# Retention's loads and steps put in another order, output zeros written later, token lists built in steps

## The chip, the core and the metric

One core of a Trainium2 chip runs the whole program. The metric is the device time of one execution in microseconds (us); of the kernel before three timed runs are at hand, and one profiled execution. The core has five engines that each take their instructions in order: TensorE (PE, with its weight loads PEld), VectorE (DVE), ScalarE (ACT), GpSimd (POOL) and SyncE (SP), which here only issues DMAs. Sixteen DMA engines move data.

## What is computed

Retention over 4 batches, 8 heads, 768 steps of 64 dimensions; its output, as 3072 rows of 512, goes through a soft mixture of 8 experts with 4 slots each, and then through a top-2 mixture of 8 experts. All is float32.

```python
for t in range(S):                                   # retention
    state = gamma * state + einsum('bhd,bhe->bhde', k[:, :, t], v[:, :, t])
    y[:, :, t] = scale * einsum('bhd,bhde->bhe', q[:, :, t], state)
x = y.transpose(0, 2, 1, 3).reshape(3072, 512)
# soft layer: logits x @ phi, softmax over tokens into slots, w1/relu/w2 per expert, softmax over slots back
# top-2 layer: noisy logits, the two largest per token, their softmax
for e in range(E):
    for k in range(2):
        mask = top2[:, k] == e
        out[mask] += top2_w[mask, k, None] * (relu(x[mask] @ w1[e]) @ w2[e])
```

## The kernel before

Retention works on 24 chunks of 128 steps, six for each batch. Loads go by pairs of chunks: `load_q` (L218) and `load_kv` (L232) move 512 KB each of q, k and v for chunk pair u; q goes into two of the four parts of `comp`, k and v into the four parts of `raws`. A load of k and v fills 128 partitions; its first 64 belong to the first chunk of the pair. `spread` (L241) copies k (ACT, two instructions of 64 partitions) and scales v (POOL, two) for one chunk. `k_t` transposes k on PE and ACT copies it to `kT`; `q_t` transposes half of a pair's q and DVE multiplies it with decay factors (two instructions); `qk` makes the scores (PE) and DVE masks them (`am`); `inter` is the product of q with the state `sbd`; `kv` updates the state (PE, then ACT copies it to `sbd`); `y_out` (the last product, L320) ends a chunk and DVE writes `XT`; `x_n` transposes it. `group0` to `group2` make the logits and slot sums for four chunks. `put` ties each step behind the one before it on PE, so the order in which the code calls the steps is the order on PE. On the other engines a list scheduler chooses the order when the kernel is built: each instruction has the priority of its place in the code and is placed when its operands and its slot are free by the scheduler's own reckoning; after that the order is fixed. `after(...)` ties instructions behind a given one on the same engine. A tile in a pool has a number of buffers (`bufs`); the next user of a buffer waits for the last accessor of the one before.

The loop over j (L438) takes chunk j, but k_t for chunk j + 2, spread for j + 3. In each step from j = 1 to 19 one or two quarters (512 KB) of the soft layer's W1 are requested on SP, each behind a one-element DVE copy from `XT[j - 1]` that paces it (L478); 28 quarters are the experts 0 to 6. In steps 11 to 16 a write of 1 MB of zeros each, from a zero tile `zt` in the buffer of W1's expert 6, clears `out` (L483). Ahead of the loop stand the loads in the order q(0), cta (356 KB of constants), kv(0), q(1), kv(1), q(2), kv(2), all on SP, with phi on ACT; `fill` issues PE products that nobody reads, 10 of them first and 2 + 2 around the first k_t.

After the loop W1 goes through PE (L536), W2's eight loads of 2 MB wait on SP for the buffers that this frees, and the products with W2 (L600) end the soft layer. Then the router makes the two choices per token (`sels`), their ranks `rr` and blocks `blk`. V1 and V2 are the weights of the top-2 layer (2 MB for each expert); three quarters of V1[2] are requested on ACT's queue behind the write of the router's weights (L695), the last quarter on SP behind a POOL copy (L979, L980).

The top-2 layer takes for each expert up to 6 full blocks of 128 tokens and one of 64, in three groups. `lists` (L747) makes the token list of one expert: comparisons on DVE, two products on POOL, 24 small matmuls (L762). `lists_all` makes the lists of experts 1 to 7 together in two passes i = 0, 1, each with a comparison table `oh` (three DVE instructions), a product `bta` on DVE and one on POOL, and 24 matmuls (L798). `fetch` gathers the tokens' rows (POOL, indirect DMA), `turn` transposes them, `hidden` makes the hidden values (PE L891, ACT relu L894, DVE rest L896 into `hhl`), `main` the output blocks of 24 matmuls (L924 to L926), evacuated by ACT into `yo` (three buffers, L933), and `add_rows` adds them to the rows of `out` with an indirect DMA on POOL (L905). Each add waits for the one before it, and the first for the zeros. `split_hi` and `split_lo` divide V2 into two parts (`wh` on ACT, `wl` on DVE). `HOOK` runs a function ahead of one matmul of one block: g_rest, the products with the last quarter of V1[2], at block 0 of expert 0, seventh step; the joint lists' two passes at blocks 1 and 2 of expert 0, where the gathers of expert 1 follow. V2[1] comes in quarters on SP, one after each of the first blocks (L944).

## Time and profile before

| | us |
|---|---|
| timed runs | 593.89, 594.40, 596.17 |
| median of the three | 594.40 |
| profiled execution | 598.08 |
| its span, first to last instruction | 596.2 |

| stage | from to, us |
|---|---|
| retention | 0 to 161 |
| soft layer's products | 161 to 204 |
| router, first list and gathers | 204 to 228.5 |
| expert 0 | 228.5 to 285.5 |
| experts 1 to 7 | 285.5 to 581 |
| last adds and end | 581 to 596 |

The page gives an engine's busy time over the whole span; the stages have different limits, so the table by stretches and the waits are read next. PE's clock has two levels here, 1.2 and 2.4 GHz; the profile gives it as a share of the higher, so 0.50 is the lower and a mean between the two says how long each was granted. An entry in square brackets behind an instruction says how long its engine stood idle before it and what ended that.

### The profile page before, as it was taken

What the parts mean: (1) busy time and instruction counts of PE and PEld (TensorE: products, weight loads), DVE (VectorE), ACT (ScalarE), POOL (GpSimd) and SP (SyncE); (2) the same over time, 40 slices, a digit from 0 to 9 for tenths busy, and PEclk for the clock granted to TensorE, in tenths of its full rate; (3) what the DMA queues carried; (4) which work ended last, traced back from release to release, by engine and by line L of the source; (5) the groups of instructions that cost most, each with busy time, mean ns of one, the idle gap of its engine ahead of it and who ended that gap; (6) DMA issues with size and microseconds to landing.
All of it is one profiled execution on the core that took longest, in us unless ns stands there. A gap on an engine that the chain in (4) does not pass through costs nothing. (4 is left out here: it accounts for less than half of the span.)

```text
span 596.2 us, 10652 instructions
## 1 busy us (share of the span) xinstructions
PE 551.9 (93%) x4176; PEld 418.9 (70%) x4176; DVE 254.6 (43%) x521; ACT 242.4 (41%) x529; POOL 224.0 (38%) x214
## 2 busy tenths in 40 slices
PE   6899999699899888799999999999999999999990
PEld 3787878578553345677787787787787787787870
DVE  3467777375303177834425225235235234324200
ACT  3565746344202235325426246256345345334200
POOL 3434634141103055445344434435344345432331
PEclk9799999799899898989999999999999999999996
DMA  9999999996699962446567566566656653644232
GB/s 251 246 273 308 236 323 379 349 349 236 257 384 410 379 211 68 96 96 167 131 138 186 109 146 181 109 149 181 128 141 174 133 122 55 138 101 51 38 40 33
DMA packets 79453, 111.76 MB, mean 187 GB/s; under 512 B 10034, under 2 KB 51570, under 8 KB 78498
## 3 DMA queue, kind: packets, MB, share of 16 engines
q1 hardware_dynamic: 65488, 94.75, 49.3%
q0 software_dynamic: 9696, 14.37, 17.4%
q10 hardware_dynamic: 4210, 1.87, 1.1%
q8 instruction: 35, 0.57, 0.4%
q14 instruction: 24, 0.20, 0.1%
HBM read 87.92 MB, written 20.41 MB: 182 GB/s over the span
## 5 line engine op out<-in xcount | busy, mean ns | idle before, releaser
L924 PE MATMUL pyc<-wh,hhl 128*128 128x512 f32 x384 | 154.1, 401 | 0.2 <-issue 0.2
L926 PE MATMUL pyc<-wh,hhl 128*128 128x512 f32 x384 | 152.4, 397 | 0.0
L925 PE MATMUL pyc<-wl,hhl 128*128 128x512 f32 x384 | 150.8, 393 | 0.0
L905 POOL DMA_INDIRECT out_dram<-yo,lsa x49 | 77.2, 1576 | 159.7 <-DMA out_dram<-yo,lsa 35.9
L896 DVE SCALAR_TENSOR_TENSOR hhl<-phc,hhl 128x512 fp32r<-128x512 f32 (+1 forms) x128 | 66.8, 551 | 73.9 <-ACT hhl L894 68.6
L926 PEld LDWEIGHTS pyc<-wh,hhl 128*128 128x128 f32 x384 | 72.4, 189 | 16.9
L925 PEld LDWEIGHTS pyc<-wl,hhl 128*128 128x128 f32 x384 | 72.6, 189 | 15.3
L924 PEld LDWEIGHTS pyc<-wh,hhl 128*128 128x128 f32 x384 | 72.3, 188 | 15.2 <-issue 0.8
L933 ACT ACTIVATE yo<-pyc,cg 128x512 f32<-128x512 f32 x48 | 33.0, 688 | 117.5 <-PE pyc L926 108.7
L872 DVE TENSOR_TENSOR wl<-w,wh 128x1024 fp32r<-128x1024 f32 x32 | 39.1, 1225 | 56.3 <-ACT wh L866 56.3
L894 ACT ACTIVATE hhl<-phc 128x512 fp32r<-128x512 f32 (+1 forms) x128 | 58.9, 515 | 10.2 <-PE phc L891 9.0
L838 POOL DMA_INDIRECT cg<-ctab,lsa x49 | 51.9, 1059 | 19.7 <-issue 13.5
L866 ACT CAST wh<-w 128x1024 fp32r<-128x1024 f32 x32 | 33.5, 1049 | 35.6 <-DMA w<-in_moe_w_dram 27.7
L296 DVE TENSOR_TENSOR am<-pa,cta 128x512 f32<-128x512 f32 x48 | 33.1, 692 | 31.3 <-PE py L320 15.9
L254 POOL TENSOR_TENSOR comp<-raws,cta 64x512 f32<-64x512 f32 x24 | 24.9, 1038 | 46.9 <-PE py L320 29.0
L274 DVE TENSOR_TENSOR qT<-pt,cta 64x512 f32<-64x512 f32 x48 | 33.0, 688 | 21.4 <-PE pt L269 21.0
L891 PE MATMUL phc<-cts,gs 128*128 128x256 f32 (+1 forms) x192 | 36.6, 300 | 3.0 <-DVE hhl L896 1.8
L254 POOL TENSOR_TENSOR vl<-raws,cta 64x512 f32<-64x512 f32 x24 | 24.9, 1038 | 34.7 <-PE py L320 22.4
L891 PEld LDWEIGHTS phc<-cts,gs 128*128 128x128 f32 x192 | 29.4, 191 | 10.3 <-issue 3.4
L292 PE MATMUL pa<-qT,kT 64*128 64x128 f32 x384 | 29.0, 292 | 1.2 <-ACT kT L283 1.2
L292 PEld LDWEIGHTS pa<-qT,kT 64*128 64x128 f32 x384 | 24.3, 194 | 5.6 <-issue 4.0
L310 PE MATMUL py<-qT,sbd 128*128 128x128 f32 x160 | 22.5, 285 | 4.9 <-ACT sbd L337 4.9
(191 smaller groups left out, 684.1 us busy)
## 6 DMA issues: line engine op xcount, KB each, us to landing
w<-in_moe_w_dram SPq DMA_DIRECT2D x77, 512.0 KB
w<-in_moe_w_dram SPq DMA_DIRECT2D x11, 2048.0 KB
comp<-in_q_dram SPq DMA_DIRECT2D x12, 512.0 KB
raws<-in_k_dram SPq DMA_DIRECT2D x12, 512.0 KB
raws<-in_v_dram SPq DMA_DIRECT2D x12, 512.0 KB
out_dram<-w SPq DMA_DIRECT2D x6, 1024.0 KB
gs<-gr SPq DMA_DIRECT2D x112, 32.0 KB
w<-in_moe_w_dram SPq DMA_DIRECT2D x2, 1024.0 KB
```

The source lines that it names most:

```text
L254: pool_ins[0] = nc.gpsimd.tensor_tensor(VL[j][rs], RAW[u][1][gs, :, r, :], gv[gs, r, t, :, None].to_broadcast([64, H, D]), op=OP.mult)
L292: mm = nc.tensor.matmul(pa[s][:, hp, :], KT[j][r, hp, :], QT[t][r, hp, g, :], start=True, stop=True)
L838: nc.gpsimd.indirect_dma_start(out=cg[:rows(b), i, :], out_offset=None, in_=ctab, in_offset=index(e, b, rows(b)))
L866: ins = nc.scalar.copy(wh, V2[e][:, 1024 * i:1024 * i + 1024])
L872: nc.vector.tensor_tensor(wl, V2[e][:, 1024 * i:1024 * i + 1024], WH[e][i], op=OP.subtract)
L891: nc.tensor.matmul(ph[:, w * i:w * i + w], GS[e][:, kf + i], CT[e, g][:, :w], start=True, stop=True)
L894: relu.append(nc.scalar.activation(h[:, :, :w], pv, AF.Relu))
L896: last = nc.vector.scalar_tensor_tensor(h[:, :, w + t0:w + t0 + 2 * P], pv[:, :, :2 * P], 0.0, h[:, :, :2 * P], op0=OP.max, op1=OP.subtract)
L905: nc.gpsimd.indirect_dma_start(out=out, out_offset=index(e, b, n), in_=y, in_offset=None, bounds_check=N - 1, oob_is_err=False, compute_op ...
L924: nc.tensor.matmul(py, hhl[:, kf, ts], wh, start=(kf == 0), stop=False)
L925: nc.tensor.matmul(py, hhl[:, kf, ts], wl, start=False, stop=False)
L926: nc.tensor.matmul(py, hhl[:, kf, tl], wh, start=False, stop=(kf == KF - 1))
```

## The change

Retention: the loads start with k, v of pair 0 in two halves of 64 partitions each (q(0) is issued between the first halves of k and v), then pair 1, then q(1); cta goes to ACT's queue, phi later. The four fills around the first k_t are dropped. Chunk 0 is run ahead of the loop through y_out, with qk(1) behind it; the loop begins at j = 1, takes k_t for chunk j + 1, spread for j + 2 and the k and v loads in the same place early in the step; steps 1 and 2 take both halves of a q pair. W1's quarters go over steps 3 to 20.

Zeros: the six writes leave the loop. `zt` is now a tile of 4 KB per partition, written by POOL; a one-element DVE operation on it reads the last gathered rows of expert 0; behind it one DMA on SP writes all of `out`.

V1[2]: its three quarters go to SP, behind an ACT copy that reads `wsl`.

Lists: expert 1 gets a list of its own by `lists`, behind the first hidden products, so its gathers no longer wait for the joint lists, which now serve experts 2 to 7. `lists_all` is cut into steps, one after each of the blocks 1 to 5 of expert 0 and 0 of expert 1; a one-element ACT copy from that block's `yo` into each tile (`mark`) holds the step's DVE instructions until then. Both `bta` products are on DVE. The two passes of matmuls go to block 4 of expert 0 and block 1 of expert 1, and the gathers of expert 2 follow the second.

```diff
-WP = 19
-Z0, ZN = 11, 6
+WP = 21
+W0, ZW = 3, 2 * DM
...
-        def load_kv(u):
+        def load_kv(u, part=None):
...
+            ps = slice(0, P) if part is None else slice(64 * part, 64 * part + 64)
...
+                nc.sync.dma_start(x[ps].rearrange("p h r d -> p h (r d)"),
+                                  src[b, :, 256 * t:256 * t + 256, :].rearrange("h (p r) d -> p h (r d)", r=2)[ps])
+                if u == 0 and part == 0 and src is k:
+                    load_q(0)
...
-        load_q(0)
-        nc.sync.dma_start(cta, csta)
-        load_kv(0)
-        nc.scalar.dma_start(phis, phi.rearrange("(k p) s -> p k s", p=P))
+        nc.scalar.dma_start(cta, csta)
+        load_kv(0, 0)
+        load_kv(0, 1)
+        load_kv(1)
         load_q(1)
-        load_kv(1)
         spread(0)
+        put(k_t, 0)
         for s in range(2):
             put(q_t, 0, s)
-        fill(psA, "py", FU)
-        put(k_t, 0)
-        fill(psA, "py", FV)
         load_q(2)
         spread(1)
         load_kv(2)
+        nc.scalar.dma_start(phis, phi.rearrange("(k p) s -> p k s", p=P))
         put(qk, 0)
         put(k_t, 1)
+        put(inter, 0)
+        put(kv, 0)
+        put(y_out, 0)
         spread(2)
-        put(q_t, 1, 0)
-        for j in range(NCH + 1):
+        put(qk, 1)
+        for j in range(1, NCH + 1):
             t, g = divmod(j, 2)
             if j < NCH:
 
+                if j + 1 < NCH:
+                    put(k_t, j + 1)
                 if j + 2 < NCH:
-                    put(k_t, j + 2)
+                    spread(j + 2)
+                if g and t + 3 < NT:
+                    load_kv(t + 3)
                 put(inter, j)
-                tn, s = (t + 1, 1) if g == 0 else (t + 2, 0)
-                if tn < NT:
-                    put(q_t, tn, s)
+                qs = [(1, 0), (1, 1)] if j == 1 else [(2, 0), (2, 1)] if j == 2 else [(t + 2, 0) if g else (t + 1, 1)]
+                for tn, s in qs:
+                    if tn < NT:
+                        put(q_t, tn, s)
...
-                if Z0 <= j < Z0 + ZN:
-                    with after(w_dma):
-                        a = NCH // ZN * (j - Z0)
-                        nc.sync.dma_start(ov[:, a:a + NCH // ZN, :],
-                                          zt[:, None, :].to_broadcast([P, NCH // ZN, DM]))
...
+            for i in range(28 * (j - W0) // (WP - W0), 28 * (j + 1 - W0) // (WP - W0)) if W0 <= j < WP else ():
+                s, dst, src = load_w1(i)
+                nc.vector.tensor_copy(dst[0:1, 0:1], XT[j - 1][0:1, 0, 0:1])
+                nc.sync.dma_start(dst, src)
...
         with after(put):
-            for i in range(KD - 1):
-                nc.scalar.dma_start(V1[2][:, 1024 * i:1024 * i + 1024], v1p[:, i])
+            nc.scalar.copy(V1[2].rearrange("p (k n) -> p k n", k=KD)[0:1, :KD - 1, 0:1], wsl[0:1, :KD - 1, 0:1])
+        for i in range(KD - 1):
+            nc.sync.dma_start(V1[2][:, 1024 * i:1024 * i + 1024], v1p[:, i])
...
     def lists_all():
+
+        def mark(ap, y):
+            nc.scalar.copy(ap, y[0:1, 0:1])
...
+        y = yield
         bm = cc.tile([P, NCH, E, LB], F16, name="bma", bufs=1)
+        mark(bm[0:1, 0, 0, 0:1], y)
...
-                eng = nc.gpsimd if a else nc.vector
-                eng.tensor_tensor(bt[:, :, a], bm, sb[:, a, :, :, None].to_broadcast([P, NCH, E, LB]), op=OP.mult)
+                mark(bt[0:1, 0, a, 0, 0:1], y)
+                nc.vector.tensor_tensor(bt[:, :, a], bm, sb[:, a, :, :, None].to_broadcast([P, NCH, E, LB]), op=OP.mult)
...
-        for e in range(1, E):
+        for e in range(2, E):
             LS[e] = ls[:, e]
+        for g in range(G):
+            fetch(2, g)
...
+            PACE.pop((e, b), tuple)(*[yo][:(e, b) in PACED])
...
+    PACED = (0, 1), (0, 2), (0, 3), (0, 4), (0, 5), (1, 0)
...
+            zt = cc.tile([P, ZW], I32, name="zt", bufs=1)
+            nc.gpsimd.memset(zt, 0)
+            nc.vector.tensor_single_scalar(zt[0:1, 0:1], CG[0, G - 1][0:1, 0, 0:1].bitcast(I32), 0, op=OP.bitwise_and)
+            nc.sync.dma_start(out.rearrange("(p a) d -> p (a d)", p=P).rearrange("p (a d) -> p a d", d=ZW),
+                              zt.bitcast(F32)[:, None, :].to_broadcast([P, N * DM // (P * ZW), ZW]))
...
+            lists(1, cc, psC, LB)
             gen = lists_all()
             next(gen)
-            HOOK[0, 1, 4] = next, gen
-            HOOK[0, 2, 2] = listed, gen
+            for b in PACED:
+                PACE[b] = gen.send
+            HOOK[0, 4, 4] = HOOK[1, 1, 2] = next, gen
...
-            pre[0] += [(fetch, e + 1, g) for g in range(G)] if e else []
+            pre[0] += [(fetch, e + 1, g) for g in range(G)] if e != 1 else []
```

## Rows read from the trace of the kernel before

**Rows 1.** Page, parts 1 and 2: engine totals; busy tenths in 40 slices
```profile
PE 551.9 (93%) x4176; PEld 418.9 (70%) x4176; DVE 254.6 (43%) x521; ACT 242.4 (41%) x529; POOL 224.0 (38%) x214
...
DMA  9999999996699962446567566566656653644232
```

**Rows 2.** Stretches: length; PE, PEld, DVE, ACT, POOL busy; clock, DMA share, GB/s
```profile
18.00:20.00 2.00, 2.00 (x14) 1.67 (x14) 0.74 (x2) 0.58 (x1) 1.87 (x3) 0.50 1.20 290
...
24.00:84.00 60.00, 58.83 (x793) 49.46 (x792) 42.19 (x81) 35.23 (x72) 27.14 (x28) 1.00 0.95 272
...
200.00:210.00 10.00, 8.79 (x72) 5.05 (x73) 3.78 (x12) 3.67 (x5) 0.09 (x1) 0.83 1.04 397
...
250.00:260.00 10.00, 7.89 (x40) 6.61 (x41) 7.02 (x21) 4.74 (x11) 1.87 (x2) 0.66 0.40 92
...
290.00:340.00 50.00, 50.00 (x254) 39.30 (x253) 16.56 (x35) 20.88 (x48) 22.39 (x18) 1.00 0.62 138
```

**Rows 3.** Who PE waited for: total us, times, longest (104:116, then 229.6:285.4)
```profile
PE py L310 <- ACT sbd L337: 4.9, 1, 4.9
...
PE pli L798 <- DVE bta L795: 2.1, 1, 2.1
...
PE phc L891 <- DVE hhl L896: 1.8, 1, 1.8
...
PE ptc L857 <- ACT cts L850: 1.4, 1, 1.4
```

**Rows 4.** Instructions in order of time: start, length; the start
```profile
6.53 2.81 DVE L274 TENSOR_TENSOR qT<-pt,cta 64x512 f32<-64x512 f32 x4 [4.41 <-PE pt L269]
...
8.68 2.51 ACT L253 COPY comp<-raws 64x512 f32<-64x512 f32 x4 [5.01 <-DMA raws<-in_k_dram]
...
22.05 1.65 PE L320 MATMUL py<-am,comp 128*64 128x128 f32 x16
...
32.69 1.05 PE L320 MATMUL py<-am,vl 128*64 128x128 f32 x16
```

**Rows 5.** Instructions in order of time; output products 7, 8, 15, 16
```profile
60.08 1.04 PE L320 MATMUL py<-am,vl 128*64 128x128 f32 x16
...
66.17 1.05 PE L320 MATMUL py<-am,comp 128*64 128x128 f32 x16
...
104.84 1.05 PE L320 MATMUL py<-am,vl 128*64 128x128 f32 x16
...
109.32 1.24 ACT L253 COPY comp<-raws 64x512 f32<-64x512 f32 x2 [5.39 <-DMA raws<-in_k_dram]
...
117.86 1.05 PE L320 MATMUL py<-am,comp 128*64 128x128 f32 x16
```

**Rows 6.** Instructions in order of time; end of the W2 products
```profile
198.70 1.06 PE L600 MATMUL po<-w,ht 128*32 128x512 f32 x8 [0.29 <-DMA w<-in_moe_w_dram]
```

**Rows 7.** Instructions in order of time; first list to the end of expert 1
```profile
218.58 1.58 PE L762 MATMUL pli<-bt,oh 128*128 128x14 f16 x24 [2.08 <-POOL bt L755]
...
228.50 0.97 PE L891 MATMUL phc<-cts,gs 128*128 128x256 f32 x6 [0.75 <-issue]
...
229.79 0.92 POOL L838 DMA_INDIRECT cg<-ctab,ls  x1 [0.30 <-issue]
...
235.72 0.64 PE L184 MATMUL pg<-w,sotT 128*32 128x256 f32 x8
...
241.26 1.94 POOL L905 DMA_INDIRECT out_dram<-yo,ls  x1 [4.34 <-ACT w L943]
...
250.33 1.04 ACT L866 CAST wh<-w 128x1024 fp32r<-128x1024 f32 x1 [5.62 <-DMA w<-in_moe_w_dram]
...
285.51 0.69 ACT L933 ACTIVATE yo<-pyc,cg 128x512 f32<-128x512 f32 x1 [0.34 <-PE pyc L926]
...
326.60 0.69 ACT L933 ACTIVATE yo<-pyc,cg 128x512 f32<-128x512 f32 x1 [0.35 <-PE pyc L926]
```

**Rows 8.** The chain that ended last: start, length, what
```profile
561.62 4.88 DMA out_dram<-yo,lsa
```

More of the change, by code (lines that the diff above doesn't have):

```diff
@@ L408, in load_w1 @@
         def load_w1(i):
-            if i % 4 == 0 and i // 4 not in W1:
+            if i % 4 == 0:
                 W1[i // 4] = (ringp if i < 8 else ringa).tile([P, 4096], F32, name="w", tag="w")
@@ L459 @@
                     put(qk, j + 1)
-                if j % 4 == 0 and j:
+                if j % 4 == 0:
                     put(group0, j // 4 - 1)
@@ L466 @@
                 put(y_out, j)
-                if j + 3 < NCH:
-                    spread(j + 3)
-                if g == 0 and t + 3 < NT:
-                    load_kv(t + 3)
-            if j:
-                if j == NCH - 3:
-                    load_w(W1, w1, E - 1, nc.sync, ringr)
-                if j == NCH - 2:
-                    load_w(W2, w2, 0, nc.sync, ringb)
-                for i in range(28 * (j - 1) // WP, 28 * j // WP if j <= WP else 0):
-                    s, dst, src = load_w1(i)
-                    nc.vector.tensor_copy(dst[0:1, 0:1], XT[j - 1][0:1, 0, 0:1])
-                    w_dma = nc.sync.dma_start(dst, src)
-                if Z0 <= j < Z0 + ZN:
-                    with after(w_dma):
-                        a = NCH // ZN * (j - Z0)
-                        nc.sync.dma_start(ov[:, a:a + NCH // ZN, :],
-                                          zt[:, None, :].to_broadcast([P, NCH // ZN, DM]))
-                if j == 8:
-                    with after(pool_ins[0]):
-                        load_small()
+            if j == NCH - 3:
+                load_w(W1, w1, E - 1, nc.sync, ringr)
+            if j == NCH - 2:
+                load_w(W2, w2, 0, nc.sync, ringb)
+            for i in range(28 * (j - W0) // (WP - W0), 28 * (j + 1 - W0) // (WP - W0)) if W0 <= j < WP else ():
+                s, dst, src = load_w1(i)
+                nc.vector.tensor_copy(dst[0:1, 0:1], XT[j - 1][0:1, 0, 0:1])
+                nc.sync.dma_start(dst, src)
+            if j == 8:
+                with after(pool_ins[0]):
+                    load_small()
         ictx.close()
@@ L800, in lists_all @@
                                  start=(i == 0 and c == 0), stop=(i == 1 and c == NCH - 1))
+            if i == 0:
+                y = yield
         lt = cc.tile([P, E, LB], F32, name="lta", bufs=1)
@@ L825 @@
     CG, HOOK = {}, {}
-    def listed(gen):
-        next(gen)
-        for g in range(G):
-            fetch(1, g)
     def fetch(e, g):
@@ L944, in main @@
                 nc.sync.dma_start(t[:, s], src[:, s])
-    feed = {}
+    feed, PACE = {}, {}
+    PACED = (0, 1), (0, 2), (0, 3), (0, 4), (0, 5), (1, 0)
     LAST = []
```

38 lines of the change are left out of this document (18 added, 20 removed).

## The prediction

> **What bounds the kernel now.** I read the page's engine totals first: TensorE (PE) is busy for 93% of the span and the 16 DMA engines are near full only in the first third [rows 1]. A change that takes no PE work away can therefore win only where PE stands still or runs at its lower clock, so I went on to the table by stretches [rows 2] and to the list of what PE waited for [rows 3]. From 24 to 84 us PE is busy 58.83 of 60 us at full clock: the retention loop is bound by PE, and ordering its steps anew is worth nothing there. The same holds from 290 us on, where 50 of 50 us are busy. Three places are left.
>
> The first is the start: chunk 0's output product begins only at 22.05 us [rows 4], and PE works at the lower level, 1.2 GHz, around 18 to 20 us [rows 2]. The second is one gap in chunk 16. ScalarE (ACT) sat 5.39 us for k's load, and since ACT takes its instructions in order, the copy into sbd stood behind it and PE waited 4.9 us for that [rows 3, 5]. Output products 15 and 16 are 13.02 us apart where 7 and 8, the same place in a group of four, are 6.09 apart: 6.9 us are lost. The third is expert 0 of the second layer: its last full block is evacuated at 285.51 and expert 1's at 326.60, a pace of 41.1 us [rows 7], while expert 0's first hidden product starts at 228.50, 57 us for the same blocks.
>
> The total is made against the profiled execution, 598.08 us (span 596.2 and 1.9 around it). The three timed runs have a median of 594.4, 3.7 us less. I carry the saved microseconds over to the median; if the 3.7 us is time by which the load in chunk 16 was later under the profiler, that much of the second term is not there to win, and the range allows for it.
>
> **Part 1, zeros out of the loop.** Six writes of 1 MB leave chunks 11 to 16. A chunk takes (66.17 - 32.69) / 6 = 5.58 us [rows 4, 5]. Per chunk the loop reads 0.786 MB of q, k and v; these alone ran at 290 GB/s [rows 2], 2.71 us. W1 adds 28 x 0.524 / 19 = 0.773 MB; rows of weights ran at 397 GB/s [rows 2], 1.95 us. A zero write of 1.049 MB at the same rate is 2.64 us. With zeros the transfers need 7.3 us per chunk of 5.58, over six chunks 10.3 us too much; without them 4.7 us. That the one late load falls into just those chunks fits. After the change W1 goes over 18 chunks, 2.05 us, together 4.76 of 5.58 us: still room. I count the whole 6.9 us, with 3.2 (less the 3.7 above) as the lower bound. The later stages do not swallow it: the W2 loads that end the first layer, where PE waits for a load [rows 6], are set off by slots that retention and the W1 products free, so they move with it.
>
> **Part 2, the start.** Before k's first load came in at 8.68 us [rows 4], 1.61 MB were asked for, which at 290 GB/s is 5.55 us, so a fixed 3.1 us stands ahead of the flow. In the new order the first half of k lands at about 5.4 us, q(0) at 7.5 (ct, cta, half of k and q, 1.28 MB), k and v of pair 1 at 13.8, q(1) at 15.7 (3.64 MB). VectorE (DVE) began its four q multiplications at 6.53, about 1 us after q came in (by the same flow), and needed 2.81 us [rows 4]; now it ends at 11.3 and the score product can begin at 11.4. Now kv and the output of chunk 0 follow at once: a score product of some 1.2 us and two mask products, each like one of the q multiplications (0.7), put output 0 at 14.1, 8 us earlier. But chunk 1 now stands behind q(1): qk(1), k_t(2), inter(1) and two q_t take PE to 19.2, DVE's four operations to 21.4, then qk(2) and kv put output 1 at 23.3, and output 2, with a q_t more than a usual chunk, at 29.4. It was at 32.69 [rows 4]. The new order has one k_t less done by then, some 0.7 us like the other four-transpose steps, so 2.6 us remain. The two dropped fills cover idle time only, but they end PE's standing still; if the work up to output 1 runs at the lower level as at 18 to 20 us before, some 2 us are lost again. Bounds 0 and 4.5 us (the gain of output 1, 22.05 + 5.58 - 23.3); I take 2.6. The issue of cta's load moves to ACT, which is idle until k comes.
>
> The Trainium skill speaks against the halves: "SBUF — State Buffer", section "Door 1: The DMA port swizzle", says that a transfer's bandwidth depends on how many of 16 ports its partitions reach, and 64 partitions reach eight. By that, four halves of 0.262 MB at half the 290 GB/s would need 7.2 us in place of 3.6, the start would win nothing, and the sum would be 9.4 in place of 13.0 us. No row of before has a 64-partition load; I leave it out of the sum, and it lies within the range.
>
> **Part 3, lists in steps.** In expert 0 PE waited 1.8 us for hhl, 2.1 for bta and 1.4 for cts, which came late because the gathers of expert 1 waited for the joint lists [rows 3]; from 250 to 260 us PE's mean clock was 0.66 [rows 2], that is 6.8 us at the lower level, 3.4 us lost. Together 8.7 us. Against that stand 24 more list matmuls for expert 1, 1.58 us as those of expert 0 were [rows 7]; DVE's and POOL's share of them runs beside PE, and 13 one-element ACT copies are off its path. 7.1 us is thus the most. What takes the place: ACT waited 5.62 us, to 250.33, for the first quarter of expert 1's V2 [rows 7], just while the list step held PE. With the list gone PE reaches the next hidden products sooner and stands before the same ACT. I take half, 3.5 us; lower bound -2.
>
> **Part 4, zeros after the gathers.** A one-element DVE operation waits for the last gather, issued until 230.71 [rows 7], so about 232; then SP starts all 6.29 MB. At 397 to 290 GB/s they need 16 to 22 us and end at 248 to 254. DMA is below half full there [rows 1, 2], so nothing is lost in bytes. Queued behind the wait on DVE are the hhl splits of expert 0's first group, if the scheduler puts it ahead of them: 0 to 2.5 us. Behind the write on SP's queue: the copies of gs (wanted 40 us later) and the V2 quarter, whose landing at about 250 stays where it was. The first add of rows into out, at 241.26 [rows 7], now waits until 248 to 254. Three yo buffers and two PSUM banks hold blocks of 5.6 us; the fourth block is due about 257, and add 0, whose transfer takes 4.88 us [rows 8], some 5.6 by my estimate with the issue of the next, ends at 254 to 260. So I count nothing, and up to 2 us at the upper end. The backlog of two adds melts: seven adds of an expert take some 37 us (six of 5.6 and a half one), its blocks 41.1.
>
> **Part 5, V1[2].** Its three loads go from ACT's queue to SP's, which has nothing waiting between expert loads and gs copies. A copy that waits for wsl takes their place on ACT, ahead of cnt and the wh casts, 0 to 0.2 us. The chain to the first gather ran through the list matmuls behind POOL [rows 7], not through ACT: nothing.
>
> Sum: 2.6 + 6.9 + 3.5 = 13.0 us, 594.4 - 13.0 = 581.4.
>
> **Rivals.** (a) All of part 3 and the upper end of part 2 come true: 4.5 + 6.9 + 7.1 = 18.5, 575.9 us. For it: the pacing follows blocks and leaves DVE free for hhl. Against: ACT's wait. (b) The zeros make the V2 quarter or the adds late, ACT stands and PE with it: part 3 is used up and up to 4 us more go, 594.4 - 9.5 + 0 to 4, about 587. For it: ACT's 5.62 us shows that there is no reserve. (c) The change does not cure the gap in chunk 16, since W1's denser pace and not the zeros delays k: 594.4 - 6.1 = 588.3. Against: from 24 to 84 us, without zeros, PE never waited for a load. (d) Slower: the last quarter of V1[2] (used by PE at 235.72 [rows 7]) stands behind the zeros in SP's queue. PE takes its work in order, so it would wait for 248 to 254 plus 1.5 us, 14 to 20 us, and run at the lower level after it (1.7 us), while part 3's gain vanishes in the wait: -9.5 + 17 + 1.7 is 9 us, about 603. It decides from a wait of 8 us (9.5 less 1.7). Against: that load waits only for a POOL copy just after the gathers' issue, the zeros for their landing.
>
> **How the numbers follow.** Forecast 0.60, (a) 0.13, (b) 0.12, (c) 0.05, (d) 0.10. The range reaches from 1.9 us below (a), 574.0, over (b) and (c) to 591.0, where the lower bounds of two terms meet (0 in the start, 3.2 in the gap) and the third wins next to nothing: 594.4 - 3.4. A measurement of this kernel can tell about 0.5%, 3 us. Faster by more than that, below 591.4: all but (d) and a remainder of bad cases, 0.85; within it 0.06; slower 0.09.
>
> **What would show it.** Output product 2 near 29.4 and no wait of ACT for k in chunks 11 to 17 (outputs 15 and 16 about 6.1 us apart); the W2 end and everything to 229 earlier by about 9.5; expert 0 some 53.5 us long in place of 57; one write of 6 MB ending 16 to 22 us after the last gather; no wait of PE at the hook of the last V1[2] quarter. Wrong would make it: a wait for yo or for V2 on ACT over 6 us, a DVE step of the lists that still stands before hhl, or chunk 1 waiting for q(1) past 24 us.

## The result and the profile after

| | before | after |
|---|---|---|
| median of 11 runs each, us | 596.17 | 599.62 |
| lowest and highest | 593.89, 599.27 | 596.22, 602.54 |
| ratio, 95% interval | | 1.0059 (1.003 to 1.0088) |
| profiled execution (span) | 598.08 (596.2) | 601.89 (600.1) |

The change makes the kernel slower by 0.6%; I had forecast 581.4 us, 2.2% faster. Ratios, here and below, leave out executions in which the cores of a die ran longer at a lower clock (four of ten in e12 below), so one can lie below that of the medians, and e5, whose profiled execution is one of them, has empty cells.

First, where in the span the time went. The milestones are the start of chunk 23's output product, the end of retention proper, and the starts of three evacuations into `yo`: blocks (0,0), (1,0) and (2,0), the first of experts 0, 1 and 2. All are read from the instructions in order of time.

| us | before | after | difference |
|---|---|---|---|
| start to output 23 | 153.32 | 145.76 | -7.56 |
| output 23 to block (0,0) | 86.98 | 90.77 | +3.79 |
| (0,0) to (1,0), expert 0 | 51.74 | 43.65 | -8.09 |
| (1,0) to (2,0), expert 1 | 43.13 | 59.78 | +16.65 |
| (2,0) to the end | 261.03 | 260.14 | -0.89 |

Up to the start of expert 1 the changed kernel is 11.9 us ahead; by the start of expert 2 it is 4.8 behind. The stretches of the trace after (columns as in [rows 2]) show both:

```profile
200.00:210.00 10.00, 7.91 (x80) 3.80 (x79) 8.26 (x24) 2.77 (x8) 5.30 (x10) 0.87 0.67 201
210.00:224.00 14.00, 13.03 (x77) 7.13 (x77) 8.32 (x13) 6.68 (x16) 10.41 (x13) 0.50 0.34 119
225.00:240.00 15.00, 14.14 (x82) 10.54 (x81) 7.25 (x17) 5.18 (x12) 6.43 (x7) 0.89 1.02 403
250.00:260.00 10.00, 10.00 (x48) 7.70 (x47) 6.17 (x11) 3.71 (x15) 4.33 (x3) 1.00 0.56 136
290.00:340.00 50.00, 36.87 (x187) 29.04 (x186) 14.08 (x32) 17.29 (x43) 20.67 (x19) 0.86 0.46 109
```

The stretch from 250 to 260, where PE was busy 7.89 us at clock 0.66 before [rows 2], is now full at full clock. The stretch from 290 to 340, which was full, has lost 13 us. The list of PE's waits (line that waited, who released it, total, times, longest) names one long wait that was not there before, and the gap's line, ACT sbd with 4.9 us [rows 3], is gone; the waits for qT are the start's and come back in the part on the prediction:

```profile
PE ptc L862 <- ACT st L856: 13.1, 1, 13.1
PE pt L344 <- DVE qT L275: 2.3, 2, 1.1
PE pt L344 <- DVE xT L324: 1.3, 3, 0.4
PE pa L293 <- DVE qT L275: 1.3, 2, 1.0
PE pli L757 <- POOL bt L750: 1.1, 2, 0.9
```

`ptc` is the transposing of gathered rows, here of expert 2's first group. The rows that lead there, on four engines, the joint lists' last instruction first and then the rest in order of time:

```profile
288.86 0.21 DVE L812 TENSOR_TENSOR lsa<-lta,pli 128x56 int32<-128x56 f32 x1
...
245.73 1.64 POOL L910 DMA_INDIRECT out_dram<-yo,ls  x1 [0.30 <-issue]
250.91 1.72 POOL L910 DMA_INDIRECT out_dram<-yo,ls  x1 [3.54 <-DMA out_dram<-yo,ls]
256.67 2.48 POOL L910 DMA_INDIRECT out_dram<-yo,ls  x1 [4.03 <-ACT hhl L899]
268.03 1.56 POOL L910 DMA_INDIRECT out_dram<-yo,ls  x1 [8.72 <-DMA out_dram<-yo,ls]
276.59 1.43 POOL L910 DMA_INDIRECT out_dram<-yo,ls  x1 [5.06 <-issue]
280.76 1.59 POOL L910 DMA_INDIRECT out_dram<-yo,ls  x1 [2.75 <-issue]
287.75 2.40 POOL L910 DMA_INDIRECT out_dram<-yo,ls  x1 [5.40 <-ACT wh L871]
294.26 1.56 POOL L910 DMA_INDIRECT out_dram<-yo,ls  x1 [4.11 <-issue]
301.51 1.43 POOL L910 DMA_INDIRECT out_dram<-yo,ls  x1 [5.69 <-DMA out_dram<-yo,ls]
303.24 1.03 POOL L843 DMA_INDIRECT cg<-ctab,lsa  x1 [0.30 <-issue]
...
308.41 0.27 ACT L855 CAST cts<-cg 128x96 fp32r<-128x96 f32 x1 [12.13 <-DMA cg<-ctab,lsa]
...
311.36 0.74 PE L862 MATMUL ptc<-identr,st 128*128 128x128 f32 x3 [13.13 <-ACT st L856]
```

The joint lists are ready at 289.07. But in POOL's fixed order the gathers of expert 2 stand behind the seven adds of expert 0 and the two of expert 1's block (1,0) and half block, and those run late: the first add goes at 245.73, 9.2 us after its block was evacuated (236.53), and eight steps later the ninth goes at 301.51, 7.0 us a step. So the gathers are issued 14.2 us after their list was ready; ACT, in order, waits 12.13 us for them, and PE 13.13. The wait costs more than itself: PE comes out of it at clock 0.50, and until about 316.7 a matmul takes 0.63 us where it then takes 0.39. By my estimate from these 5.3 us at half speed that is another 2.6 us.

```profile
313.00:315.00 2.00, 2.00 (x6) 1.56 (x5) 0.00 (x0) 0.00 (x0) 0.69 (x1) 0.50 0.64 188
```

From these rows came theory 1: the held zeros make the adds late, the list steps put expert 2's gathers behind those adds, and only the two together stop PE. Theory 2: the joint lists are simply made too late. Theory 3: the held zeros alone cost it, whatever the lists.

### The profile page after: what moved, and what is told of

It is laid out like the page before. It is cut to its first block, busy times and chain, and to the rows that moved or that the text cites. A ratio compares the mean times of both kernels' runs of the same rounds, so it can differ in the third digit from the quotient of the medians.

```text
span 600.1 us, 10722 instructions
## 1 busy us (share of the span) xinstructions
PE 556.8 (93%) x4196; PEld 422.7 (70%) x4196; DVE 256.0 (43%) x530; ACT 243.4 (41%) x543; POOL 224.3 (37%) x214
## 3 DMA queue, kind: packets, MB, share of 16 engines
q1 hardware_dynamic: 64192, 95.96, 48.5%
## 5 line engine op out<-in xcount | busy, mean ns | idle before, releaser
L930 PE MATMUL pyc<-wl,hhl 128*128 128x512 f32 x384 | 153.5, 400 | 0.0
L910 POOL DMA_INDIRECT out_dram<-yo,lsa x42 | 66.4, 1581 | 136.4 <-ACT w L949 36.2
L843 POOL DMA_INDIRECT cg<-ctab,lsa x42 | 45.0, 1071 | 13.5 <-issue 12.9
L910 POOL DMA_INDIRECT out_dram<-yo,ls x14 | 23.8, 1696 | 56.2 <-issue 26.8
L255 POOL TENSOR_TENSOR comp<-raws,cta 64x512 f32<-64x512 f32 x24 | 24.9, 1038 | 40.6 <-issue 14.2
```

The costliest lines, as they stand in the source:

```text
L255: pool_ins[0] = nc.gpsimd.tensor_tensor(VL[j][rs], RAW[u][1][gs, :, r, :], gv[gs, r, t, :, None].to_broadcast([64, H, D]), op=OP.mult)
L843: nc.gpsimd.indirect_dma_start(out=cg[:rows(b), i, :], out_offset=None, in_=ctab, in_offset=index(e, b, rows(b)))
L910: nc.gpsimd.indirect_dma_start(out=out, out_offset=index(e, b, n), in_=y, in_offset=None, bounds_check=N - 1, oob_is_err=False, compute_op ...
L930: nc.tensor.matmul(py, hhl[:, kf, ts], wl, start=False, stop=False)
```

## The experiments

Each table cell below is worked out as in the table above, from the run's own profiled execution; the ratio is that to the kernel before on the same chip. "23" is output 23.

| run | median | ratio, interval | to 23 | 23 to (0,0) | expert 0 | expert 1 |
|---|---|---|---|---|---|---|
| e1 gathers first | 589.64 | 0.9868 (0.9802, 0.9934) | 146.13 | 91.15 | 42.89 | 49.00 |
| e2 no zeros | 589.63 | 0.9889 (0.9838, 0.9941) | 146.57 | 88.19 | 48.48 | 44.82 |
| e3 zeros in loop | 592.46 | 0.9927 (0.9892, 0.9961) | 149.82 | 87.54 | 47.50 | 44.83 |
| e4 old lists | 593.76 | 0.9929 (0.9888, 0.9970) | 147.61 | 84.50 | 56.81 | 43.12 |
| e5 retention only | 597.06 | 0.9962 (0.9922, 1.0002) | | | | |
| e6 late zeros only | 592.70 | 0.9945 (0.9917, 0.9972) | 146.45 | 86.69 | 55.09 | 43.14 |
| e7 gathers, V2 first | 587.37 | 0.9853 (0.9799, 0.9907) | 143.97 | 89.87 | 42.95 | 45.49 |
| e8 third of zeros early | 589.78 | 0.9889 (0.9824, 0.9953) | 144.94 | 94.05 | 42.81 | 45.62 |
| e9 lists only | 596.34 | 0.9972 (0.9938, 1.0006) | 153.68 | 93.14 | 43.10 | 46.84 |
| e10 start order | 590.42 | 0.9840 (0.9779, 0.9901) | 149.68 | 88.41 | 42.92 | 49.47 |
| e11 start, full loads | 591.14 | 0.9877 (0.9819, 0.9934) | 150.92 | 87.88 | 42.90 | 46.84 |
| e12 zeros and lists | 600.87 | 0.9978 (0.9924, 1.0033) | 145.93 | 87.58 | 42.88 | 60.60 |
| e13 q(1) first | 590.90 | 0.9886 (0.9832, 0.9939) | 145.28 | 91.58 | 42.85 | 45.13 |
| e14 q(1) first, full loads | 589.25 | 0.9821 (0.9740, 0.9901) | 145.68 | 89.45 | 42.96 | 45.86 |

### The new wait: e1, e2, e4, e12

**e1**: the changed kernel with POOL's order made by hand.

```diff
...
+        hold = []
         for g in range(G):
-            fetch(2, g)
+            with after(*hold):
+                hold = [fetch(2, g)]
+            if HELD:
+                with after(*hold):
+                    hold = [add_rows(*HELD.pop(0))]
...
-            add_rows(e, b, yo[:r], r)
+            if (e, b) in ((1, 0), (1, SB)):
+                HELD.append((e, b, yo[:r], r))
+            else:
+                add_rows(e, b, yo[:r], r)
...
```

> The changed kernel with one thing else: on GpSimd's queue the gathers of expert 2's first group stand ahead of the adds of blocks (1,0) and (1,5), and those adds go between the three groups' gathers. Lists, zeros and retention stay as changed. Theory 1 (the 13.1 us wait of TensorE for expert 2's gathers comes from the adds that stand ahead of them on GpSimd): the wait falls to 0 to 4 us, and the time from 599.6 to about 587 (583 to 592). Theory 2 (the joint lists themselves come too late, wherever the adds stand): the wait stays over 9 us and the time within 596 to 601. If ScalarE then waits for a free yo buffer since two adds come later, 3 to 6 us of the gain are given back there.

The lists are ready at the same time as in the changed kernel (289.41 against 289.07), but the gathers go out at once (the lists' last instruction, then POOL):

```profile
289.20 0.21 DVE L812 TENSOR_TENSOR lsa<-lta,pli 128x56 int32<-128x56 f32 x1
...
286.71 1.57 POOL L916 DMA_INDIRECT out_dram<-yo,ls  x1 [5.09 <-issue]
289.68 1.02 POOL L848 DMA_INDIRECT cg<-ctab,lsa  x1 [1.41 <-DVE lsa L812]
```

PE's wait falls from 13.1 to 2.4 us (its waits from 285 to 345):

```profile
PE ptc L868 <- ACT st L862: 2.4, 1, 2.4
```

The time falls by 10 us to 589.6, the first layer's and the lists' work being unchanged. Theory 2 falls: the lists were in time, the gathers were not. As expected, a part is given back: the adds are as late as before, ACT waits 5.4 us for a `yo` buffer at 293.27, and expert 1 takes 49.00 us where it took 43.13 in the kernel before.

**e2**: the changed kernel without the write of zeros; the clearing of `out` is left out. Gathers stay behind the adds.

```diff
...
-            nc.sync.dma_start(out.rearrange("(p a) d -> p (a d)", p=P).rearrange("p (a d) -> p a d", d=ZW),
-                              zt.bitcast(F32)[:, None, :].to_broadcast([P, N * DM // (P * ZW), ZW]))
```

> The changed kernel without the write of zeros into out (the clearing of out is left out; no add has to wait for it). Theory 1a (the gathers of expert 1 that stand ahead of the first add hold the adds back as much as the zeros do): first add at about 243 instead of 245.7, the adds from 256 to 276 somewhat quicker, the wait for expert 2's gathers still 6 to 12 us, time 592 to 598. Theory 3 (the held zeros alone make the backlog of adds): first add right behind the first evacuated block at about 238, the wait under 3 us, time 583 to 588.

The first add goes at 238.25, as theory 3 said. The gathers of expert 2 still stand behind nine adds, but go out at 292.91, 1.4 us after their list is ready (291.48), and PE does not wait for them: from 290 to 340 it is busy for 50.00 of 50 us. Taking the zeros away cures as much as turning the order round, so both are needed for the 13 us; with adds on time, POOL's order costs nothing here. Part of the earlier first add is the build's doing: with no zeros to wait for, the scheduler puts it ahead of expert 1's last two gathers on POOL, and in the changed kernel it stands behind them.

What e2 gains there it loses in part in expert 0 (48.48): ACT waits 4.3 us for the first quarter of V2[1], which stands behind 29 copies of gs on SP, and PE 3.9 us for expert 1's gathered rows, whose casts stand behind it on ACT (ACT, then PE):

```profile
250.38 1.05 ACT L871 CAST wh<-w 128x1024 fp32r<-128x1024 f32 x1 [4.32 <-DMA w<-in_moe_w_dram]
...
255.71 0.56 PE L862 MATMUL ptc<-identr,st 128*128 128x128 f32 x3 [3.90 <-DVE st L857]
```

So the time, 589.6, lies between the two ranges that I had stated.

**e4**: the changed kernel with the lists of before (joint lists for experts 1 to 7), zeros held.

```diff
-            lists(1, cc, psC, LB)
             gen = lists_all()
             next(gen)
-            for b in PACED:
-                PACE[b] = gen.send
-            HOOK[0, 4, 4] = HOOK[1, 1, 2] = next, gen
+            HOOK[0, 1, 4] = next, gen
+            HOOK[0, 2, 2] = listed, gen
...
```

> The changed kernel with the lists as before: the joint lists serve experts 1 to 5 and expert 2's gathers are issued with their own blocks; start, load order and held zeros stay as changed. Theory 1 and 2 both: no wait of 13 us before expert 2, since its lists are there early; expert 0 is again slow (1.8 us for hhl, 2.1 for bta, 1.4 for cts, as in the kernel before), so the 4.3 us that the steps gained are lost: time 586 to 591. Theory 3 (the held zeros cost it): the adds are late here too and TensorE waits over 6 us for what stands behind them, time 594 to 600.

No long wait ahead of expert 2: expert 1 takes 43.12. Expert 0 takes 56.81, 5.1 more than before, and PE's longest wait there is 4.4 us, for hhl behind a late gather of expert 1 (e6 shows the rows). With late zeros the old lists' expert 0 gets slower, not much more than that; theory 3, which has the whole loss come from the zeros, falls. The time, 593.8, lies between the range of theories 1 and 2 and that of theory 3.

**e12**: the kernel before with held zeros and list steps, but its own start and loads. It completes the pair e6 and e9, in which each stands alone; its edit is those two together.

> The kernel before with the zeros held until the first gathers have landed and the lists in steps, but with the start and the loads of before. Alone, the held zeros took 3.6 to 4.6 us off and the steps about 2. If they add up: about 591. Theory 1 (late zeros put the adds behind, and the steps' list puts expert 2's gathers behind those adds): TensorE waits 9 to 14 us for expert 2's gathers at about 300 us and the time is 598 to 604, above the kernel before, with no part of the new load order in it. If the wait needs the new load order too, it is under 5 us here.

PE's longest waits from 230 to 345, the same as in the changed kernel, with none of the new load order:

```profile
PE ptc L858 <- ACT st L852: 12.2, 1, 12.2
PE phc L892 <- issue: 1.1, 1, 1.1
```

The mechanism is as theory 1 has it. PE's wait for expert 2's gathers is 13.1 and 12.2 us in the two runs that have both held zeros and list steps with the gathers behind the adds, at most 2.4 in the seven with the gathers ahead of them (e1, e7, e8, e10, e11, e13, e14), at most 0.4 in the three with steps but no late zeros (e2, e3, e9), and none is seen in the two with late zeros and the old lists (e4, e6). The price in time is less sure: the median (600.87) is where it was expected, the ratio (0.9978) is lower and its interval holds 1. The ratio lies above that of the zeros alone (0.9945), but the intervals overlap; that the pair is worth less than the zeros alone is seen in the trace (expert 1 takes 60.60 us against 43.14 in e6) and not shown by the times.

### What each part is worth: e3, e5, e6, e9

**e6**: the kernel before with one change, the zeros out of the loop and held. They go in rows of 2 KB, as before, where the changed kernel's have 4 KB (e12 likewise).

```diff
-                if Z0 <= j < Z0 + ZN:
...
+            nc.vector.tensor_single_scalar(zt[0:1, 0:1], CG[0, G - 1][0:1, 0, 0:1].bitcast(I32), 0, op=OP.bitwise_and)
+            nc.sync.dma_start(out.rearrange("(p a) d -> p (a d)", p=P).rearrange("p (a d) -> p a d", d=ZW),
...
```

> The kernel before with one change: the zeros leave the loop and are written after the first gathers have landed. If the zeros made the gap in chunk 16: outputs 15 and 16 are 6 to 6.5 us apart and the last output of the first layer is at 146 to 147. If held zeros cost expert 0 what they cost with the old lists in the new order (blocks (0,0) to (2,0) 99.9 us apart against 94.9 before), 5 us of it are given back and the time is 593 to 596. If they cost nothing there, as I forecast: 588 to 590. If the gap does not go: over 599.

Output products 15 and 16, in order of time (before: 104.84 and 117.86 [rows 5]):

```profile
104.87 1.05 PE L320 MATMUL py<-am,vl 128*64 128x128 f32 x16
110.97 1.04 PE L320 MATMUL py<-am,comp 128*64 128x128 f32 x16
```

The gap is gone, and retention ends 6.87 us earlier: the second term of my sum, to the tenth. Of this expert 0 gives 3.4 back (55.09 against 51.74): held zeros are not free there even with the old lists. One add now stands among the seven gathers of expert 1 on POOL, ACT waits for the rows of a gather behind it, and PE for the hhl that ACT makes after that, a chain like that of the changed kernel on a smaller scale; how much of it is the add and how much a slower landing was not settled (ACT, then PE):

```profile
263.30 0.24 ACT L841 CAST cts<-cg 128x64 fp32r<-128x64 f32 x1 [5.55 <-DMA cg<-ctab,lsa]
...
265.48 0.60 PE L882 MATMUL phc<-cts,gs 128*128 128x320 f32 x1 [3.94 <-ACT hhl L885]
```

The ratio of 0.9945 is 3.3 us of 597.

**e3**: the changed kernel with the zeros back in chunks 11 to 16. **e5**: the same with the old lists too, so that only start, loads and V1[2] are new.

```diff
-                nc.sync.dma_start(dst, src)
+                w_dma = nc.sync.dma_start(dst, src)
+            if Z0 <= j < Z0 + ZN:
+                with after(w_dma):
...
```

> The changed kernel with the zeros back in the loop, six writes in chunks 11 to 16 as before; start, load order and list steps stay as changed. If the zeros in the loop caused the gap in chunk 16 (ScalarE's wait for k), it is back: outputs 15 and 16 are 11 to 13 us apart in place of 6.2, which costs 5 to 7 us; if the new order of k's loads cured it, they stay 6 to 7 apart. The second layer then goes as without the zeros: theory 1a has the 13.1 us wait at 6 to 12 us (time 597 to 602 with the gap, 592 to 597 without), theory 3 under 3 us (time 590 to 594 with the gap, 583 to 588 without).

> The new start, load order and V1[2] on SyncE's queue, but zeros in the loop (chunks 11 to 16) and the lists as in the kernel before. If the order of the loads is worth what the run with zeros in the loop showed (last output of the first layer at 149.8 us against 153.3 before) and nothing later swallows it: last output at 149 to 150.5, time 3 to 4 us under the kernel before, 592 to 593.5; then the list steps, which that run had besides, are worth 0 to 1 us in sum. If the list steps are worth the 3.5 us that I forecast, this run is at 595 to 597 and the first layer's gain is lost in between.

In e3 the gap is back one chunk later and smaller: outputs 16 and 17 are 8.70 us apart against 4.67 in the changed kernel, since ACT waits again for k (3.9 us, line by line of ACT's waits from 104 to 122):

```profile
ACT comp L255 <- DMA raws<-in_k_dram: 3.9, 1, 3.9
```

So the zeros made the gap, and the new order of the loads, with W1's new pace, makes it smaller but does not close it. Start and loads by themselves (e5) are at 0.9962, 2.3 us, with 1 just inside the interval; e3 against e5 puts the list steps at 0.35%, 2 us, with intervals that overlap.

**e9**: the kernel before with the list steps alone.

```diff
+            lists(1, cc, psC, LB)
             gen = lists_all()
             next(gen)
-            HOOK[0, 1, 4] = next, gen
-            HOOK[0, 2, 2] = listed, gen
+            for b in PACED:
+                PACE[b] = gen.send
+            HOOK[0, 4, 4] = HOOK[1, 1, 2] = next, gen
...
```

> The kernel before with one change: the joint lists made one step per block, with expert 1's own list ahead of them; zeros stay in the loop, start and loads as before. If the steps are worth what I forecast: blocks (0,0) to (2,0) 91 to 92 us apart in place of 94.9, time 592 to 594. If they are worth what the two runs with zeros in the loop suggest (92.3 with the steps, 96.8 without): a gain of 2 to 3 us. Since the zeros have landed long before, the adds are not backlogged and TensorE waits under 5 us for expert 2's gathers even though they stand behind the adds (theory 1); if the list itself is too late (theory 2), it waits over 8 us and the time is 598 or more.

0.9972, 1.7 us, with 1 inside the interval. PE waits 0.4 us for expert 2's gathers, which stand behind the adds here too, as theory 1 said for adds that are on time. The table says why it isn't more: expert 0 gains 8.6 us (43.10 against 51.74), more than the 7.1 that I had called the most; but the time from output 23 to (0,0) is 90.0 on average over the twelve runs with steps against 86.1 over the three without (before, e4, e6), and expert 1 with the second pass in it takes 45 to 49 (leaving out the two runs with the long wait) against 43.1. Of the first, 1.6 us are the 24 list matmuls of expert 1, which now run inside the first block; where the rest comes from I did not settle, because in that stage the granted clock falls at another place in each run. In the changed kernel the whole loss lies between the first hidden product, which at 220.76 is 7.7 us earlier than before (228.50 [rows 7]), and the evacuation of block (0,0) 15.8 us later (11.8 before).

### Making it faster: e7, e8

**e7**: e1, and the first quarter of V2[1] on SP ahead of expert 2's sixteen gs copies.

```diff
-                nc.sync.dma_start(t[:, s], src[:, s])
+                ins = nc.sync.dma_start(t[:, s], src[:, s])
+            if (e, b) == (0, 0):
+                with after(ins):
+                    g_copy(2, REST[0], 0)
...
-        g_copy(2, g_split(pg2, 1), 0)
+        REST.append(g_split(pg2, 1))
```

> The run with the gathers of expert 2 ahead of the adds, and besides the first quarter of expert 1's V2 issued on SyncE's queue ahead of the sixteen copies of gs for expert 2. Theory 1 in its full form (the backlog of adds is held up by the late zeros, not by V2): ScalarE's wait for V2 goes under 1 us but TensorE gains little, time 587 to 590, wait for yo buffers still 5 to 8 us. If the bunched V2 loads are what makes the adds slow: adds between 256 and 280 us no longer 8 to 9 us apart, time 584 to 587.

587.4 us, below both kernels; e1 and e7 are not told apart by their intervals. The first add is as late as before (244.61, its block at 233.84), but six steps of adds take 36.1 us, in place of 42.0 in the changed kernel and 38.7 in e1, and PE's wait for expert 2's gathers is 0.5. One step is still 9.2 us (261.84 to 271.06). DMA issues by kind, count and median us from issue to landing, for the first seven adds in the changed kernel (244 to 292), in e1 (246 to 290) and in e7 (244 to 284):

```profile
out_dram<-yo,ls POOLq DMA_INDIRECT x7, 5.8
```

```profile
out_dram<-yo,ls POOLq DMA_INDIRECT x7, 6.2
```

```profile
out_dram<-yo,ls POOLq DMA_INDIRECT x7, 4.7
```

ACT waited only 1.5 us for that quarter in e1, so the wait itself was not what cost. Between e1 and e7, which differ in nothing else, an add's landing falls from 6.2 to 4.7 us: the loads bunched behind the gs copies are one of the things that slowed the adds.

**e8**: e7, with a third of the zeros sent at about 203 us behind the last weights of the first layer.

```diff
         load_w(V1, v1, 1, nc.sync, ringv)
...
+        nc.sync.dma_start(ov[:, :ZK], ze[:, None, :].to_broadcast([P, ZK, DM]))
...
```

> As the run before it, and a third of the zeros (2.1 MB) goes out right behind the last weights of the first layer (about 203 us, where the DMA engines are mostly idle until the gathers), the rest after the first gathers have landed. Theory 1 (backlog from the late zeros): the zeros have landed by about 239, the first add goes at 239 to 242 in place of 246 to 248, ScalarE waits under 3 us for yo buffers in experts 0 and 1, TensorE under 3 us for expert 2's gathers; time 583 to 587. If the early third delays V1[2] or the first gathers, expert 0 begins 2 to 5 us later and the time is that of the run before it or worse, 588 to 592.

The first add goes at 241.82, and experts 0 and 1 take the same as in e7 (42.81 and 45.62), so with gathers and V2 first an earlier end of the zeros buys nothing. Block (0,0) comes 4 us later after output 23 than in e7, and the time, 589.8, is in the range that I had given to an early third that delays what follows (the intervals do not tell it from e7). PE was at clock 0.50 from 232 to 236 in e8, at 1.00 in e7, so this can be the clock and need not be the early third.

### The start: e10, e11, e13, e14

Over seven profiles with the changed start (after, e1 to e4, e7, e8) output 2 comes at 30.21 to 33.88, 32.1 on average; with the old start (before, e6, e9, e12) at 31.89 to 32.70, 32.4 on average. The 2.6 us that I forecast are not there. Four runs on top of e7 asked why.

**e10** puts chunk 1's `kv` and `y_out` ahead of q(1)'s transposes and x_n between the two steps of q. **e11** is e10 with k and v of pair 0 in one piece each.

```diff
                 put(inter, j)
+                if j == 1:
+                    put(kv, j)
+                    put(y_out, j)
...
                     if tn < NT:
                         put(q_t, tn, s)
+                    if j < 3 and s == 0:
+                        put(x_n, j - 1)
```

```diff
-            ps = slice(0, P) if part is None else slice(64 * part, 64 * part + 64)
+            ps = slice(0, P)
...
-        load_kv(0, 1)
```

> The run with the gathers first and V2's first quarter first, and a start in which chunk 1's mask product and output product stand ahead of q(1)'s transposes, and in chunks 1 and 2 the transposes of x stand between the two steps of q (in the changed kernel both steps of q come first, and TensorE waits 2.1 to 2.3 us for VectorE's four multiplications behind them). If that wait and chunk 1 standing behind q(1) is what ate the start's gain: output 1 at 18 to 21 us in place of 23.5 to 25.7, output 2 at 28 to 30 in place of 30.2 to 33.9 (at the same granted clock), time 2 us under the run without it, 585 to 586. If only the clock in the first 30 us decides: output 2 still at 30 to 34, time 587 to 590.

> As the run before it, with k and v of the first pair loaded in one piece each (128 partitions, q behind k) in place of two halves of 64 partitions. In the changed kernel the halves moved 215 to 231 GB/s from 8 to 12 us where the kernel before moved 290. If the halves cost bandwidth: all later loads land about 1 us sooner (q(1) transposed about 1 us sooner), while chunk 0's first k comes 1 to 1.5 us later; output 0 at 15 to 16.5, output 2 about 1 us sooner than in the run before it; time within 1.5 us of it. If they don't: output 0 is 1 to 2 us later and output 2 no sooner.

Output 1 comes at 19.34, but output 2 at 35.92: the copy of x stands on ACT behind k's copies for pair 2, which wait for their load, and PE waits 3.0 us for the copy's slot; from 28 to 32 us it then runs at clock 0.50. The new order only moved the wait. In e11 the stretches from 8 to 12 us move 280 and 290 GB/s, in e10 221 and 231, so the halves do cost bandwidth; output 0 is only 0.5 us later, but output 2, which was to come about 1 us sooner, comes at 37.10.

**e13** is e7 with q(1)'s load ahead of v of pair 1, **e14** is e13 with pair 0 in one piece each.

```diff
-                if u == 0 and part == 0 and src is k:
-                    load_q(0)
+                if u < 2 and not part and src is k:
+                    load_q(u)
...
-        load_q(1)
```

> The run with the gathers and V2 first, and q(1)'s load put ahead of v of pair 1 on SyncE's queue, nothing else. In the runs with the changed start the third output came 11.8 us after q(1)'s transposes where TensorE kept its full clock in between, and 13.3 us where it did not, whenever q(1) came (18.4 to 22.1 us). If q(1)'s landing sets the start: transposes of q(1) at 16 to 17 us, output 2 at 28 to 30, time 585 to 586. If the clock or VectorE sets it: output 2 at 30 to 33, time 587 to 589.

> As the run before it, with k and v of the first pair in one piece each. If the halves cost bandwidth as the run with full loads suggested (280 to 290 GB/s from 8 to 12 us in place of 221 to 231): q(1)'s transposes 1 to 1.5 us sooner than in the run before it, output 0 about 0.5 us later, output 2 at 27 to 29, time 584 to 586. If output 0 sets the pace, it is 0.5 to 1 us slower than the run before it.

Output 2 comes at 31.44 and 31.94: q(1)'s landing does not set it alone. In e13 PE only gets to q(1) at 19.64, being late since chunk 0; in e14 it waits 3.0 us for ACT's kT, again behind a copy that waits for a load. In each of the four another wait took the place of the one that was shortened, and none brought output 2 below e7's 30.21; what the start would need is not shown. The four runs lie at 0.982 to 0.989, like e7; they do not tell a gain over it.

## Why the prediction was wrong

**Part 1, zeros out of the loop: right.** Forecast 6.9, measured 6.87 alone (e6), and in the changed kernel 7.56 less the start's 0.7. The cause is confirmed by e3.

**Part 2, the start: mis-sized.** Forecast 2.6 from output 2 at 29.4; measured 31.99 in the changed kernel, a gain of 0.7, and 0.3 as a mean. Output 0 came at 14.22 (forecast 14.1), but then output 1 at 24.19 (23.3) and 2 another 7.80 us later (6.1). The rows show what was missing, PE at the lower level in part (an output product takes 1.92 us where it takes 1.05 at the full clock; the granted clock is 0.50 from 24 to 26 us), and PE waiting for DVE's four multiplications where both steps of q stand in one chunk (2.3 us in all):

```profile
19.28 2.81 DVE L275 TENSOR_TENSOR qT<-pt,cta 64x512 f32<-64x512 f32 x4 [0.63 <-PE pt L270]
...
20.82 0.63 PE L344 MATMUL pt<-ct,xT 128*128 128x128 f32 x4 [1.13 <-DVE qT L275]
...
24.19 1.92 PE L321 MATMUL py<-am,comp 128*64 128x128 f32 x16
...
29.82 0.63 PE L344 MATMUL pt<-ct,xT 128*128 128x128 f32 x4 [1.14 <-DVE qT L275]
```

I had named the clock as a risk. In chunk 1 DVE's four multiplications were in my sum, but ended at 22.1 and not at 21.4; in chunk 2 I had added one q_t and no wait for DVE, and PE waited 1.1 us. (The upper bound of this part, 22.05 + 5.58 - 23.3, is 4.3 and not 4.5.)

**Part 3, lists in steps: right in size for expert 0, too high in sum.** Forecast 3.5, measured about 2 (1.7 alone, 2 by e3 against e5, neither clear of the noise). Expert 0 gains 8 to 9 us where V2 is in time, and about 7 of them go elsewhere: 3.9 on average ahead of block (0,0) and some 3 into expert 1. I had priced only 1.6 us of list matmuls and one wait for V2.

**Part 4, zeros after the gathers: the step that failed.** "So I count nothing, and up to 2 us at the upper end. The backlog of two adds melts: seven adds of an expert take some 37 us ... its blocks 41.1." The write itself was as forecast: the stretch 225 to 240, in which it falls, moved 403 GB/s, and in e4, where its landing is on record, it took 19.0 us from its issue (16 to 22 forecast). The first add went at 245.73, behind the zeros and also behind expert 1's last gathers, which wait on POOL for a slot until block (0,1) is out:

```profile
242.62 0.94 POOL L843 DMA_INDIRECT cg<-ctab,ls  x1 [4.35 <-ACT yo L938]
243.87 1.55 POOL L843 DMA_INDIRECT cg<-ctab,ls  x1 [0.30 <-issue]
```

Then the seven adds took 48.5 us (245.73 to 294.26) and not 37; the adds issued from 245 to 295 took 4.9 to 10.6 us to land, 6.1 in the median, and not 4.88. The blocks of expert 0 came in 43.65 us. The backlog grew. The loads stood there by the change too: I had the first quarter of expert 1's V2 stay where it was, but SP issued it at 256.58, 10.7 us later than before: 28 gs copies stood right ahead of it and took 31.8 us, and one of them waited 5.4 us for the zeros (SP's queue, before and then after):

```profile
245.84 0.53 SPq L944 DMA_DIRECT2D w<-in_moe_w_dram  x1
```

```profile
256.58 38.65 SPq L950 DMA_DIRECT2D w<-in_moe_w_dram  x11
```

And the step asked only what an add's lateness does to `yo`. (ACT did wait for `yo`, 14.5 us in four times, the longest 5.8, and PE's list shows no wait behind it.) POOL also issues the gathers, and the change itself moves expert 2's gathers behind the second list pass and so behind adds that run late. I listed what is queued behind the new wait on DVE and on SP and not what is queued behind the adds on POOL: 13.1 us. With the gathers first (e1) the change is worth 1.3%, with V2 first too (e7) 1.5%: 586 us on the scale of the forecast, inside its range of 574 to 591. On that scale the changed kernel is at 597.9, 16.5 us from the forecast. The wait and the lower clock behind it, 15.7 together, are most of that; the 1.9 of the start and the 1.5 of the lists are within what the runs leave open. That PE runs at the lower level after a long wait was a term of rival (d), at 1.7; in part 4, where the wait came, nothing stood for it.

**Part 5, V1[2]:** no run has it alone, but PE's list shows no wait at its hook, as forecast; the last quarter's load stood ahead of the zeros on SP, so rival (d) did not happen. That the kernel came out slower, which I gave to (d) alone, had another cause. Rival (b), late adds, was the right direction: I gave it "up to 4 us" and 0.12, where it was 13.

## What to carry over

When a transfer is made to wait, follow the first instruction that needs it onto its engine's queue, and list everything behind it there for as long as the backlog lasts, above all what the same change has just moved onto that queue. A backlog melts only by the difference between what feeds the queue and what serves it; take the serving time from rows in which the queue is backed up and the same loads run beside it. Two parts that each look like a gain alone can cancel each other: run them alone and as a pair.

## What was not expected of the hardware

**Loads of 64 partitions ran at about three quarters of the bandwidth.** Stretches 8 to 10 and 10 to 12 us, e13 with halves, then e14 with whole loads (last column GB/s):

```profile
8.00:10.00 2.00, 1.89 (x8) 1.48 (x8) 0.92 (x2) 0.09 (x1) 0.45 (x1) 1.00 1.23 205
10.00:12.00 2.00, 1.49 (x8) 1.49 (x9) 1.84 (x3) 1.10 (x2) 1.63 (x2) 1.00 1.21 213
```

```profile
8.00:10.00 2.00, 1.76 (x8) 1.05 (x6) 1.21 (x2) 0.58 (x1) 0.00 (x0) 1.00 1.21 278
10.00:12.00 2.00, 1.50 (x11) 1.32 (x12) 1.92 (x4) 0.00 (x0) 1.31 (x2) 1.00 1.20 290
```

205 and 213 against 278 and 290 GB/s, at the same share of busy engines. The prediction weighed a page of the Trainium skill here, "SBUF — State Buffer", section "Door 1: The DMA port swizzle", by which 64 partitions reach half of the ports. Its sign is borne out; these runs show 0.74, in a stretch that can hold whole loads too.

**PE took 1.8 times as long for the same work while the granted clock read 1.00.** The same eight transposes took 1.09 us in e7 and 1.97 in e13, and the granted clock of both stretches (8 to 10 us) is 1.00 (e7's is below, e13's above). In order of time, e7, then e13:

```profile
7.67 1.09 PE L270 MATMUL pt<-ct,comp 128*128 128x128 f32 x8 [0.98 <-DMA comp<-in_q_dram]
...
8.00:10.00 2.00, 0.95 (x8) 0.72 (x7) 1.59 (x3) 0.00 (x0) 0.71 (x1) 1.00 1.22 211
```

```profile
7.92 1.97 PE L270 MATMUL pt<-ct,comp 128*128 128x128 f32 x8 [0.45 <-DMA comp<-in_q_dram]
```

The ratio is near that of PE's two levels, but why the column does not show it is open. Here, in the first 15 us, the length of an instruction told more than the clock's column.
